# Probabilities of twelve even heads formed by rows and turned by DMA; two DRAM buffers laid out by group

## The chip, the cores and the metric

The kernel runs on one core of a Trainium2 chip. A core has TensorE (PE in the profile, with its weight loads PEld), VectorE (DVE), ScalarE (ACT), GpSimd (POOL) and SyncE (SP), which here issues nearly all DMAs, and 16 DMA engines. Each engine works off its own queue in program order. The metric is the device time of one launch in microseconds (us), the median of several runs.

## The reference

Two independent blocks, joined along the last axis. Block A is causal attention with a compressive memory: 32 heads of 18 columns, four segments of 512 positions. Block B is the real part of a two-dimensional Fourier transform by matrices.

```
# A, for every head and each of N = 4 segments of L = 512
logits = einsum("bhqd,bhkd->bhqk", qs, ks) * scale + mask
p = softmax(logits); a_dot = einsum("bhqk,bhkd->bhqd", p, vs)
pq = phi(qs); a_mem = (pq @ M) / (pq @ z + 1e-6)
o = g * a_mem + (1 - g) * a_dot
M = M + phi(ks)^T @ vs; z = z + phi(ks).sum(0)
...
a = o.reshape(B, S, D) @ wo
# B
y = dft_seq_re @ (x @ dft_hid_re.T) - dft_seq_im @ (x @ dft_hid_im.T)
```

S = 2048, D = 576. Everything is in float32; the kernel keeps that precision by splitting values in a high and a low part.

## The kernel before

**Stages.** First the projections, segment by segment (`project_qk`, `project_v`), with the memory's sums and its lookups (`lookup`); then the attention, with the Fourier matmuls woven in; last the output product. The projections leave their results in DRAM: queries and keys in `qd` and `kd`, the values' split parts in `vd[s]`, shape [128, 4, 8, 220] (row, position block j, group of four heads, columns), and the memory's part of the output in `amd[s]`, shape [4, 128, 576]. The attention reads them back by groups: `value_load` takes `vd[s][:, :, g8]`, and `memory_load` takes 72 columns of all four blocks of `amd[s]`.

**Attention.** The 128 (segment, head) pairs are numbered n = 4 G + h, with 32 groups G of four heads; groups 0 to 7 are segment 0, and so on. A generator, `attention`, makes 68 passes p. In pass p it starts the even head 2p and, with lags, carries on older heads: the odd head 2(p - 2) + 1 is filled (`F_LAG` = 2), the even head 2(p - 3) gets its transposed scores (`T_LAG` = 3), and the heads of pass p - 4 are multiplied with the values (`V_LAG` = 4). The sets of calls of a pass stand between eight yields; I call the calls ahead of yield k "block k". After each yield, the driving loop puts Fourier matmuls (the function `dense`, mostly line 583) in TensorE's queue until their share of the planned time has caught up. `later(n, ...)` puts a call off by n yields.

**An even head** goes the way by columns. `s_fill` computes its scores by rows, and DVE takes the rows' maxima from them as minima of the negated scores (line 964). `maxima` (POOL) splits the maxima of a group's two even heads in three bf16 parts. `maxima_transpose` turns these on TensorE (line 1015), ACT copies them to the tile `mt` (line 1017), and two small DMAs write them under the queries as three further rows of the contraction. `t_fill` then computes the transposed scores with the maximum already taken off (lines 1032, 1035, 1040, 1041), ACT takes the exponential twice, into f16 (`phi`) and f32 (`pf`) (lines 1044, 1045), POOL masks the diagonal blocks (`t_mask`), ACT makes their f16 part (`t_hi`) and DVE and POOL the low parts `plo` (`t_lo`). The result is already laid out as `pv` needs it.

**An odd head** goes the way by rows. `f_fill` computes the scores by rows and DVE the minima; `f_exp` adds a constant to the minima on ACT (line 984) and takes the exponential with them as bias (line 987) into `pf`; `f_split_hi` (ACT, line 994) and `f_split_lo` (POOL and DVE, line 998) make a high and a low f16 part in `hl`; `f_turn` transposes both with one DMA on SyncE's queue (line 1003) into `ptt`. `pv` multiplies with the values (lines 1076, 1077), and `pv_out` (DVE) scales and adds the memory's part.

**Banks and buffers.** Scores lie in four PSUM banks: `bank(name, shape, dtype, tag)` gives the two of tag "s" or the two of tag "t" in turn. A new tile in a bank waits for all readers of the one before it. `s_fill` and the odd head's fills 1 and 2 use "s"; `t_fill` and the odd head's fill 0 use "t". In a pass with a group's maxima to turn, `t_fill(.., 1, G)` gives `maxima_transpose` the unused last quarter of its own bank; only in pass 2, where no head is that far, the maxima take a "t" bank of their own (`trm`). `pf` has three buffers, `phi`, `plo`, `ptt` and `hl` two each.

Of the kernel before, what the change touches and what calls it, by code (L numbers as in the profile page):

```python
# [23 lines left out]
P = 128  # L24
# [11 lines left out]
COPIES = ((0, 3, 2, 0), (1, 3, 2, 2), (0, 5, 1, 0), (1, 5, 1, 1))  # L36
COPY_ROWS = 144


@with_exitstack  # L40
def infini_attention_and_fnet(ctx: ExitStack, tc: tile.TileContext, xT, wqk, w8, wv, wo, beta, xtT, cT, hT, out):
# [9 lines left out]
    kd = [dram.tile([D, 6, L], BF16, name=f"kd{s}") for s in range(NSEG)]  # L51
    vd = [dram.tile([P, 4, 8, 220], BF16, name=f"vd{s}") for s in range(NSEG)]
    amd = [dram.tile([4, P, D], F32, name=f"amd{s}") for s in range(NSEG)]
    yd = [dram.tile([P, D], F32, name=f"yd{t}") for t in range(NT)]
# [254 lines left out]
    def project_v(s, j, meanwhile):  # L309
# [26 lines left out]
        pool.tensor_tensor(vs[:, :, 0:18], r, vs[:, :, 36:54], OP.subtract)  # L336
        later(1, dma, vd[s][:, j], vs.rearrange("p (g h) c -> p g (h c)", g=8))

# [51 lines left out]
    def lookup(s, j):  # L390
# [26 lines left out]
        pool.tensor_tensor(am, nd[:, :, :DH], w.to_broadcast([P, H, DH]), OP.mult)  # L417
        later(1, dma, amd[s][j], am.rearrange("p h d -> p (h d)"))
        yield
# [73 lines left out]

    def value_load(G):
        if G < NG:
            s, g8 = divmod(G, 8)
            VS[G] = sa.tile([P, 4, 220], BF16, name="vst", bufs=2)
            dma(VS[G], vd[s][:, :, g8])

# [489 lines left out]
    def f_split_hi(n):  # L989
        f = F_[n][1]  # L990
        hl = sa.tile([P, 2, 1280], F16, name="hl", bufs=2)
        F_[n][2] = hl
        for a, b in ((512, 1280), (0, 512)):
            act.activation(hl[:, 0, a:b], f[:, a:b], AF.Copy)  # L994
# [5 lines left out]
    def f_turn(n):  # L1000
        hl = F_.pop(n)[2]
        PT[n] = sa.tile([P, 20, P], F16, name="ptt", bufs=2)
        nc.sync.dma_start_transpose(PT[n], hl.rearrange("p a c -> p (a c)"))

# [56 lines left out]
    def pv(n):  # L1061
        G, h = divmod(n, 4)
        if h % 2 == 0:
            PV[n // 2] = ps.tile([P, 448], F32, name="pv", bufs=1)
        pt = PT.pop(n)
        for i in range(4):
            o = PV[n // 2][:, (h % 2 * 4 + i) * 55:(h % 2 * 4 + i + 1) * 55]
            for j in range(i + 1):
                if h % 2:
                    b = FIRST_COL[i] // P + j  # L1070
                    hi, lo = pt[:, b], pt[:, 10 + b]
# [4 lines left out]
                pe.matmul(o, hi, v, start=j == 0, stop=False)  # L1076
                pe.matmul(o[:, 18:], lo, v[:, 18:], start=False, stop=j == i)  # L1077
# [57 lines left out]
    NP = 2 * NG  # L1135
    SLOTS = (1060.0, 890.0, 1060.0, 660.0, 890.0, 1060.0, 650.0, 1210.0)

    def attention():
        for p in range(NP + V_LAG):
            def even(lag, fn, *a):  # L1140
                if 0 <= p - lag < NP:
                    fn(2 * (p - lag), *a)

            def odd(lag, fn, *a):
# [33 lines left out]
            odd(F_LAG, f_fill, 0)  # L1178
            if p % 2 and p < NP:
                maxima(p // 2)  # L1180
# [95 lines left out]
```

## Time and profile before

| | |
|---|---|
| median of 3 runs | 993.38 us (992.39 to 993.64) |
| the profiled execution | 994.13 us; its span 992.4 us; granted clock 0.999 |
| TensorE busy | 980.9 us (99%) |
| weight loads | 918.3 us |
| VectorE | 786.4 us |
| ScalarE | 714.7 us |
| GpSimd | 675.2 us |
| moved by DMA | 209.97 MB in 304351 packets, 204992 of them under 512 bytes |
| DMA transposes | 64, 3.0 to 6.3 us each on SyncE's queue |

Times within the profile are counted from the span's start. The attention's scores run from 221 us to 917 us. In the timeline a row gives the start, the length, the engine, the line and the operation, `out<-in`, and in brackets how long the engine was idle before it and what ended that. A matmul's length is longer than the time that it keeps the next one from starting, so the distance of two starts is the cost of a matmul in a full queue. For an instruction of SyncE the length is the time that its queue was busy issuing the DMA, not the transfer.

### The profile page before, as it was taken

What the parts mean: (1) busy time and instruction counts of PE and PEld (TensorE: products, weight loads), DVE (VectorE), ACT (ScalarE), POOL (GpSimd) and SP (SyncE); (2) the same over time, 40 slices, a digit from 0 to 9 for tenths busy, and PEclk for the clock granted to TensorE, in tenths of its full rate; (3) what the DMA queues carried; (4) which work ended last, traced back from release to release, by engine and by line L of the source; (5) the groups of instructions that cost most, each with busy time, mean ns of one, the idle gap of its engine ahead of it and who ended that gap; (6) DMA issues with size and microseconds to landing.
All of it is one profiled execution on the core that took longest, in us unless ns stands there. A gap on an engine that the chain in (4) does not pass through costs nothing.

```text
span 992.4 us, 25495 instructions
## 1 busy us (share of the span) xinstructions
PE 980.9 (99%) x9246; PEld 918.3 (93%) x9246; DVE 786.4 (79%) x2115; ACT 714.7 (72%) x1687; POOL 675.2 (68%) x744
## 2 busy tenths in 40 slices
PE   9999999999999999999999999999999999999998
PEld 8988989898999999999999999999999999999998
DVE  6657668584678787887898878888888898989985
ACT  6757576563888777877878788886777778788442
POOL 2657576686676667676775777767676667887561
PEclk9999999999999999999999999999999999999999
DMA  7537556777578898899999998779999999988663
GB/s 241 191 117 244 194 170 241 238 243 214 146 179 206 224 239 227 203 226 241 223 253 242 235 211 191 187 196 218 247 231 219 224 241 252 249 200 180 168 199 112
DMA packets 304351, 209.97 MB, mean 212 GB/s; under 512 B 204992, under 2 KB 259136, under 8 KB 304192
## 3 DMA queue, kind: packets, MB, share of 16 engines
q1 hardware_dynamic: 304000, 208.20, 80.9%
q8 instruction: 72, 1.18, 0.5%
q14 instruction: 55, 0.45, 0.1%
q10 hardware_dynamic: 224, 0.14, 0.0%
HBM read 122.37 MB, written 58.98 MB: 183 GB/s over the span
## 4 chain that ended last, share of the span: by engine, by line
PE 84%; DVE 7%; ACT 4%; DMA 2%; issue 2%; POOL 1%; SPq 0%; POOLq 0%; DVEq 0%; ACTq 0%
PE d L583 38%; PE s L958 7%; PE v L84 4%; PE pv L1076 4%; PE qk L250 4%; PE d L628 3%; PE d L629 3%; PE d L630 3%; PE t L861 2%; PE pv L1077 2%; PE m L363 1%; PE d L861 1%; PE s L861 1%; PE t L1032 1%; PE qk L84 1%
## 5 line engine op out<-in xcount | busy, mean ns | idle before, releaser
L964 DVE CUSTOM_DVE_ANT_0 s<-s,causal 128x128 f32<-128x128 f32 (+3 forms) x512 | 248.4, 503 | 94.2 <-PE s L958 85.0
L456 POOL TENSOR_TENSOR clo<-craw,chi 128x512 fp32r<-128x512 f32 x158 | 218.2, 1381 | 91.1 <-ACT chi L451 60.8
L583 PE MATMUL d<-wide,chi 128*128 128x288 f32 x1408 | 261.9, 303 | 0.2 <-DVE y L653 0.2
L583 PEld LDWEIGHTS d<-wide,chi 128*128 128x128 f32 x1408 | 210.6, 188 | 2.7 <-issue 0.7
L583 PE MATMUL d<-wide,clo 128*128 128x288 f32 x704 | 173.4, 313 | 0.0
L998 POOL TENSOR_TENSOR hl<-pf,hl 128x768 f16<-128x768 f32 x64 | 114.0, 1782 | 67.4 <-ACT hl L994 55.6
L958 PE MATMUL s<-ks,qs 108*128 108x128 bf16 (+3 forms) x512 | 132.9, 303 | 1.7 <-DVE negm L964 1.2
L1044 ACT ACTIVATE phi<-t 128x384 f16<-128x384 f32 x128 | 61.8, 483 | 100.1 <-PE t L1041 100.1
L987 ACT ACTIVATE pf<-s,nb 128x128 f32<-128x128 f32 (+3 forms) x256 | 128.3, 527 | 6.2
L583 PE MATMUL d<-ab,chi 128*128 128x288 f32 x640 | 123.3, 302 | 0.0
L1059 DVE TENSOR_TENSOR plo<-pf,phi 128x384 f16<-128x384 f32 (+1 forms) x128 | 122.3, 955 | 0.0
L583 PEld LDWEIGHTS d<-wide,clo 128*128 128x128 f32 x704 | 117.8, 189 | 1.4
L1045 ACT ACTIVATE pf<-t 128x384 f32<-128x384 f32 (+1 forms) x192 | 99.6, 519 | 6.6 <-PE t L1032 6.3
L451 ACT ACTIVATE chi<-craw 128x512 fp32r<-128x512 f32 x160 | 100.1, 626 | 4.0 <-DMA craw<-xtT 2.4
L583 PEld LDWEIGHTS d<-ab,chi 128*128 128x128 f32 x640 | 97.8, 188 | 0.5
L994 ACT ACTIVATE hl<-pf 128x768 f16<-128x768 f32 (+1 forms) x128 | 87.4, 729 | 2.0
L583 PE MATMUL d<-ab,clo 128*128 128x288 f32 x320 | 83.0, 308 | 0.0
L628 PE MATMUL d<-wide,chi 128*128 128x288 f32 x256 | 81.4, 318 | 0.0
L630 PE MATMUL d<-wide,clo 128*128 128x288 f32 x256 | 75.6, 296 | 0.9 <-POOL clo L456 0.9
L629 PE MATMUL d<-wide,chi 128*128 128x288 f32 x256 | 75.6, 295 | 0.0
L1059 POOL TENSOR_TENSOR plo<-pf,phi 128x384 f16<-128x384 f32 x64 | 61.7, 963 | 12.0 <-ACT pf L1045 9.1
L998 DVE TENSOR_TENSOR hl<-pf,hl 128x512 f16<-128x512 f32 x64 | 69.2, 1081 | 0.0
(285 smaller groups left out, 2521.9 us busy)
## 6 DMA issues: line engine op xcount, KB each, us to landing
craw<-cT SPq DMA_DIRECT2D x128, 256.0 KB
ks<-kd SPq DMA_DIRECT2D x32, 432.0 KB
qs<-qd SPq DMA_DIRECT2D x32, 432.0 KB
craw<-xtT SPq DMA_DIRECT2D x32, 320.0 KB
vd<-vs SPq DMA_DIRECT2D x16, 440.0 KB
vst<-vd SPq DMA_DIRECT2D x32, 220.0 KB
qd<-p SPq DMA_DIRECT2D x16, 384.0 KB
kd<-p SPq DMA_DIRECT2D x16, 384.0 KB
```

The lines of the kernel that those rows point to most:

```text
L451: act.activation(hi, raw[:, :4], AF.Copy)
L456: engine.tensor_tensor(lo, raw[:, :4], hi.bitcast(F32), OP.subtract)
L583: pe.matmul(o[h], a, b[:, h * 288:h * 288 + 288], start=start, stop=stop)
L628: pe.matmul(o, xh[:, k], wl[k][:, cs], start=k == 0, stop=False)
L629: pe.matmul(o, xh[:, k], wh[k][:, cs], start=False, stop=False)
L630: pe.matmul(o, xl[:, k], wh[k][:, cs], start=False, stop=False)
L958: pe.matmul(o[:, c:c + w], q[:, i * P:w], k[:, :w], start=True, stop=True)
L964: dve.tensor_tensor_reduce(o[:, c:c + w], o[:, c:c + w], CAUSAL[0][:, L - w:], scale=scale, scalar=-LOWEST, op0=OP.add, op1=OP.min, accum_ ...
L987: act.activation(f[:, FIRST_COL[i]:FIRST_COL[i] + w], o[:, c:c + w], AF.Exp, bias=nb[:, i:i + 1], scale=-1.0)
L998: engine.tensor_tensor(hl[:, 1, a:b], f[:, a:b], hl[:, 0, a:b], OP.subtract)
L1045: act.activation(f[:, r:r + w], o[:, :w], AF.Exp, bias=LIFT, scale=SCALE)
L1059: (pool if kind == 2 else dve).tensor_tensor(lo[:, a:b], f[:, a:b], hi[:, a:b], OP.subtract)
```

## The change

The even heads (h = 0 and 2) of groups 0, 2, 4, 6, 16 and 18, twelve heads in all, go the way by rows. For them `s_fill`, `t_fill`, `t_mask`, `t_hi`, `t_lo` fall away, as do `maxima` and `maxima_transpose` for their groups; in their place stand `f_fill` (blocks 1 and 4, all three fills in "t" banks), `f_exp` (blocks 2, 3, 5), `f_split_hi` (block 5), `f_split_lo` (block 6), all in the pass of lag 3, and `f_turn` in block 1 of the next pass. Their `pv` moves from block 3 to block 6, just ahead of the odd head's. Their high and low parts lie in a buffer of tag `pf`, and each is transposed by a DMA of its own into a tile of tag `phi` or `plo`. Where the head of lag 3 goes by rows, no transposed-score bank is there to take the next group's maxima, so `maxima_transpose` takes a "t" bank of its own, ahead of the row-wise fills.

`vd` becomes [128, 8, 4, 220] and `amd` [128, 8, 4, 72], so that what a group loads is contiguous in each row, and what a projection stores is not.

```diff
+ROWWISE_GROUPS = (0, 2, 4, 6, 16, 18)
...
-    vd = [dram.tile([P, 4, 8, 220], BF16, name=f"vd{s}") for s in range(NSEG)]
-    amd = [dram.tile([4, P, D], F32, name=f"amd{s}") for s in range(NSEG)]
+    vd = [dram.tile([P, 8, 4, 220], BF16, name=f"vd{s}") for s in range(NSEG)]
+    amd = [dram.tile([P, 8, 4, 72], F32, name=f"amd{s}") for s in range(NSEG)]
...
-        later(1, dma, vd[s][:, j], vs.rearrange("p (g h) c -> p g (h c)", g=8))
+        later(1, dma, vd[s][:, :, j], vs.rearrange("p (g h) c -> p g (h c)", g=8))
...
-        later(1, dma, amd[s][j], am.rearrange("p h d -> p (h d)"))
+        later(1, dma, amd[s][:, :, j], am.rearrange("p (g h) d -> p g (h d)", g=8))
...
-            dma(VS[G], vd[s][:, :, g8])
+            dma(VS[G], vd[s][:, g8])
...
     def f_fill(n, kind):
-        o = scores(n, kind, "s" if kind else "t")
-        if kind == 1:
+        o = scores(n, kind, "s" if kind and n % 2 else "t")
+        if n not in F_:
...
     def f_split_hi(n):
         f = F_[n][1]
-        hl = sa.tile([P, 2, 1280], F16, name="hl", bufs=2)
+        hl = (sa.tile([P, 2, 1280], F16, name="hl", bufs=2) if n % 2
+              else sa.tile([P, 2, 1280], F16, name="hle", tag="pf", bufs=3))
...
     def f_turn(n):
         hl = F_.pop(n)[2]
-        PT[n] = sa.tile([P, 20, P], F16, name="ptt", bufs=2)
-        nc.sync.dma_start_transpose(PT[n], hl.rearrange("p a c -> p (a c)"))
+        if n % 2:
+            PT[n] = sa.tile([P, 20, P], F16, name="ptt", bufs=2)
+            nc.sync.dma_start_transpose(PT[n], hl.rearrange("p a c -> p (a c)"))
+            PT[n] = PT[n][:, :10], PT[n][:, 10:]
+        else:
+            PT[n] = [sa.tile([P, 10, P], F16, name="pte", tag=tag, bufs=2) for tag in ("phi", "plo")]
+            for i, t in enumerate(PT[n]):
+                nc.sync.dma_start_transpose(t, hl[:, i])
...
-            dma(OG[G % 2], amd[s][:, :, 72 * g8:72 * g8 + 72].rearrange("q p c -> p q c"))
+            dma(OG[G % 2], amd[s][:, g8])
...
+            def turned(lag, fn, *a):
+                if 2 * (p - lag) not in ROWWISE:
+                    even(lag, fn, *a)
+
+            def rowwise(lag, fn, *a):
+                if 2 * (p - lag) in ROWWISE:
+                    even(lag, fn, *a)
...
-            even(T_LAG + 1, t_lo, 0)
+            turned(T_LAG + 1, t_lo, 0)
             odd(F_LAG + 1, f_exp, 2)
             odd(F_LAG + 1, f_split_hi)
             yield SLOTS[0]
-            G = p // 2 - 1 if p % 2 == 0 and 0 < p <= NP else None
-            even(0, s_fill, 0)
-            even(T_LAG, t_fill, 0)
-            even(T_LAG, t_fill, 1, G)
-            if G is not None and p < T_LAG:
+            rowwise(T_LAG + 1, f_turn)
+            G = p // 2 - 1 if p % 2 == 0 and 0 < p <= NP and p // 2 - 1 not in ROWWISE_GROUPS else None
+            turned(0, s_fill, 0)
+            turned(T_LAG, t_fill, 0)
+            turned(T_LAG, t_fill, 1, G)
+            if G is not None and (p < T_LAG or 2 * (p - T_LAG) in ROWWISE):
                 maxima_transpose(G, bank("trm", [P, L], F32, "t"))
+            rowwise(T_LAG, f_fill, 0)
+            rowwise(T_LAG, f_fill, 1)
             odd(F_LAG + 1, f_split_lo, pool, 512, 1280)
             yield SLOTS[1]
-            even(0, s_fill, 1)
+            turned(0, s_fill, 1)
             odd(F_LAG + 1, f_split_lo, dve, 0, 512)
+            rowwise(T_LAG, f_exp, 0)
             yield SLOTS[2]
-            even(V_LAG, pv)
-            even(0, s_fill, 2)
-            even(T_LAG, t_mask)
+            turned(V_LAG, pv)
+            turned(0, s_fill, 2)
+            turned(T_LAG, t_mask)
+            rowwise(T_LAG, f_exp, 1)
             yield SLOTS[3]
             odd(F_LAG, f_fill, 1)
-            even(T_LAG, t_fill, 2)
+            turned(T_LAG, t_fill, 2)
+            rowwise(T_LAG, f_fill, 2)
             odd(F_LAG, f_fill, 0)
...
             odd(F_LAG + 1, f_turn)
...
-            even(T_LAG, t_hi)
+            turned(T_LAG, t_hi)
+            rowwise(T_LAG, f_exp, 2)
+            rowwise(T_LAG, f_split_hi)
             yield SLOTS[5]
+            rowwise(V_LAG, pv)
             odd(V_LAG, pv)
             odd(F_LAG, f_fill, 2)
+            rowwise(T_LAG, f_split_lo, pool, 512, 1280)
+            rowwise(T_LAG, f_split_lo, dve, 0, 512)
             odd(F_LAG, f_exp, 1)
-            even(T_LAG, t_lo, 1)
-            even(T_LAG, t_lo, 2)
+            turned(T_LAG, t_lo, 1)
+            turned(T_LAG, t_lo, 2)
             yield SLOTS[6]
```

More of the change, by code (lines that the diff above doesn't have):

```diff
@@ L1068, in pv @@
             for j in range(i + 1):
-                if h % 2:
+                if h % 2 or n in ROWWISE:
                     b = FIRST_COL[i] // P + j
-                    hi, lo = pt[:, b], pt[:, 10 + b]
+                    hi, lo = pt[0][:, b], pt[1][:, b]
                 else:
@@ L1131, in memory_load @@
             s, g8 = divmod(G, 8)
-            dma(OG[G % 2], amd[s][:, :, 72 * g8:72 * g8 + 72].rearrange("q p c -> p q c"))
+            dma(OG[G % 2], amd[s][:, g8])
     F_LAG, T_LAG, V_LAG = 2, 3, 4
     NP = 2 * NG
+    ROWWISE = {4 * G + h for G in ROWWISE_GROUPS for h in (0, 2)}
     SLOTS = (1060.0, 890.0, 1060.0, 660.0, 890.0, 1060.0, 650.0, 1210.0)
@@ L1160, in attention @@
             yield SLOTS[0]
-            G = p // 2 - 1 if p % 2 == 0 and 0 < p <= NP else None
-            even(0, s_fill, 0)
-            even(T_LAG, t_fill, 0)
-            even(T_LAG, t_fill, 1, G)
-            if G is not None and p < T_LAG:
+            rowwise(T_LAG + 1, f_turn)
[4 more added lines that the diff above has]
+            if G is not None and (p < T_LAG or 2 * (p - T_LAG) in ROWWISE):
                 maxima_transpose(G, bank("trm", [P, L], F32, "t"))
+            rowwise(T_LAG, f_fill, 0)
+            rowwise(T_LAG, f_fill, 1)
             odd(F_LAG + 1, f_split_lo, pool, 512, 1280)
             yield SLOTS[1]
-            even(0, s_fill, 1)
+            turned(0, s_fill, 1)
             odd(F_LAG + 1, f_split_lo, dve, 0, 512)
+            rowwise(T_LAG, f_exp, 0)
             yield SLOTS[2]
-            even(V_LAG, pv)
-            even(0, s_fill, 2)
-            even(T_LAG, t_mask)
+            turned(V_LAG, pv)
+            turned(0, s_fill, 2)
+            turned(T_LAG, t_mask)
+            rowwise(T_LAG, f_exp, 1)
             yield SLOTS[3]
             odd(F_LAG, f_fill, 1)
-            even(T_LAG, t_fill, 2)
+            turned(T_LAG, t_fill, 2)
+            rowwise(T_LAG, f_fill, 2)
             odd(F_LAG, f_fill, 0)
-            if p % 2 and p < NP:
+            if p % 2 and p < NP and p // 2 not in ROWWISE_GROUPS:
                 maxima(p // 2)
```

## The prediction

> **What bounds the kernel now.** I read the busy times first, then the stages, then TensorE's instructions in order of time, and last what the other engines wait for. The busy times and the chain of work that ended last:
>
> ```profile
> PE 980.9 (99%) x9246; PEld 918.3 (93%) x9246; DVE 786.4 (79%) x2115; ACT 714.7 (72%) x1687; POOL 675.2 (68%) x744
> ...
> PE 84%; DVE 7%; ACT 4%; DMA 2%; issue 2%; POOL 1%; SPq 0%; POOLq 0%; DVEq 0%; ACTq 0%
> ```
>
> Stages next (columns: stretch, its length, PE, PEld, DVE, ACT and POOL busy, granted clock, DMA share, GB/s):
>
> ```profile
> 300.00:350.00 50.00, 50.00 (x551) 47.07 (x550) 40.16 (x121) 39.52 (x94) 35.18 (x40) 1.00 0.84 215
> ...
> 500.00:550.00 50.00, 50.00 (x550) 46.87 (x549) 45.60 (x130) 41.16 (x98) 34.42 (x41) 1.00 1.01 246
> ...
> 600.00:650.00 50.00, 50.00 (x516) 47.55 (x515) 40.40 (x128) 41.20 (x107) 37.46 (x44) 1.00 0.79 192
> ```
>
> In the attention stage (about 220 to 915 us) TensorE is busy all the time at full clock, even where the DMA share is 1.01. So what leaves TensorE's queue is gained at its full pitch, and any wait put into that queue is lost in full. ACT is busy 39 to 41 of 50 us there: a fifth of its time is left.
>
> **What leaves TensorE.** Two stretches of its timeline, passes 28 and 29 of the attention loop:
>
> ```profile
> 514.22 0.39 PE L1032 MATMUL t<-qs,ks 111*128 111x128 bf16 x4
> 514.44 0.33 PE L1035 MATMUL t<-qs,ks 111*128 111x384 bf16 x1
> 514.60 0.22 PE L1015 MATMUL t<-ident,mb 128*128 128x128 bf16 x1
> 514.63 0.51 PE L583 MATMUL d<-wide,clo 128*128 128x288 f32 x2
> ...
> 518.35 0.22 PE L1040 MATMUL t<-qs,ks 111*128 111x128 bf16 x1
> 518.41 0.27 PE L1041 MATMUL t<-qs,ks 111*128 111x256 bf16 x1
> 518.52 0.38 PE L958 MATMUL s<-ks,qs 108*128 108x512 bf16 x1
> ```
>
> The pitch (start to next start) counts, not the duration, since matmuls overlap. An even head's transposed scores take 514.60 - 514.22 = 0.38 us and 518.52 - 518.35 = 0.17 us: 0.55 us. Its row-wise scores exist already for the maxima; they are only computed three passes later, so they count as nothing. Twelve heads: 6.6 us. The maxima's transpose (L1015) costs 0.03 us at 514.60 and is gone six times: 0.2 us. Sum: -6.8 us, and no more, because TensorE has no idle time that the change could also remove.
>
> **What ACT gets.** Groups over the attention stage (busy us, mean ns | idle before, releaser):
>
> ```profile
> L987 ACT ACTIVATE pf<-s,nb 128x256 f32<-128x256 f32 x253 | 126.8, 526 | 6.2
> L1045 ACT ACTIVATE pf<-t 128x512 f32<-128x512 f32 x189 | 98.0, 519 | 6.6 <-PE t L1032 6.3
> L994 ACT ACTIVATE hl<-pf 128x768 f16<-128x768 f32 (+1 forms) x128 | 87.4, 729 | 2.0
> L1044 ACT ACTIVATE phi<-t 128x384 f16<-128x384 f32 x126 | 60.8, 483 | 99.4 <-PE t L1041 99.4
> L1054 ACT ACTIVATE phi<-pf 128x512 f16<-128x512 f32 x63 | 39.7, 630 | 0.8 <-POOL pf L1049 0.8
> L984 ACT ACTIVATE nb<-nb 128x2 f32<-128x2 f32 x189 | 37.5, 198 | 5.1 <-DVE nb L964 4.8
> ```
>
> A head formed by columns costs ACT (98.0 + 60.8 + 39.7) / 63 = 3.2 us; one formed by rows (126.8 + 87.4 + 37.5) / 63 = 4.0 us. So ACT has 0.8 us more per head. It had an idle gap of 99.4 / 63 = 1.6 us per pass, ahead of L1044, that could hide this. But the gap stays: the exponential of the last block now waits for DVE's minimum of it, and DVE works off the odd head's block first.
>
> **The wait that the change adds.** In pass 2G + 4 of each of the six groups G, the maxima of group G + 1 can't ride in a transposed-score bank any more. `maxima_transpose` takes a "t" bank of its own, the first row-wise fill takes the other one, and the second fill needs the first one again: it waits until ACT has copied the maxima out (`mt`). That copy stands in ACT's queue behind the odd head's last exponential and both of its `f_split_hi` copies. Behind the waiting matmul stands all of TensorE's work, and nothing hides it. How late is ACT at that point? TensorE's fill against ACT's copy, for passes 4, 8, 12, 16, 36 and 40:
>
> ```profile
> 264.48 0.39 PE L1032 MATMUL t<-qs,ks 111*128 111x128 bf16 x4
> ...
> 310.76 0.39 PE L1032 MATMUL t<-qs,ks 111*128 111x128 bf16 x4
> ...
> 351.41 0.39 PE L1032 MATMUL t<-qs,ks 111*128 111x128 bf16 x4
> ...
> 392.11 0.39 PE L1032 MATMUL t<-qs,ks 111*128 111x128 bf16 x4
> ...
> 599.22 0.39 PE L1032 MATMUL t<-qs,ks 111*128 111x128 bf16 x4
> ...
> 647.69 0.39 PE L1032 MATMUL t<-qs,ks 111*128 111x128 bf16 x4
> ```
>
> ```profile
> 267.24 0.25 ACT L1017 ACTIVATE mt<-t 24x128 bf16<-24x128 f32 x1
> ...
> 313.02 0.25 ACT L1017 ACTIVATE mt<-t 24x128 bf16<-24x128 f32 x1
> ...
> 352.34 0.25 ACT L1017 ACTIVATE mt<-t 24x128 bf16<-24x128 f32 x1
> ...
> 392.54 0.60 ACT L1045 ACTIVATE pf<-t 128x512 f32<-128x512 f32 x1 [0.41 <-PE t L1032]
> 393.04 0.25 ACT L1017 ACTIVATE mt<-t 24x128 bf16<-24x128 f32 x1
> ...
> 601.10 0.25 ACT L1017 ACTIVATE mt<-t 24x128 bf16<-24x128 f32 x1
> ...
> 649.38 0.25 ACT L1017 ACTIVATE mt<-t 24x128 bf16<-24x128 f32 x1
> ```
>
> The copy no longer has an exponential of 0.5 us (392.54 to 393.04) ahead of it, and takes 0.25 us. TensorE is at the second fill about 0.25 us after the old L1032 (the maxima's matmul, and one 512-wide fill). So the wait is (copy's start) - (L1032's start) - 0.5 us: 2.3, 1.8, 0.4, 1.4 and 1.2 us, and for pass 16, where ACT idled 0.41 us, 0.0. Sum 7.1 us if ACT is as late as now. It will be later, by its 0.8 us and by the later start of the last exponential: bounds 0 us (the 1.6 us gap swallows it) and 1.8 us (0.8 us and a DVE queue of one more us). I take 1.0 us, near the added work: 6 x 1.0 = 6.0 us. Wait in all: 13.1 us.
>
> **SyncE's queue and the transposes.** Its transposes, a part of pass 8 and a store:
>
> ```profile
> L1003 SPq DMA_TRANSPOSE ptt<-hl x64: 3037/3745/6270, 258.7 to 918.4; - x64
> ```
>
> ```profile
> 211.68 0.32 SPq L94 DMA_DIRECT2D vd<-vs  x1
> ...
> 313.30 1.56 SPq L94 DMA_DIRECT2D qs<-mt  x2
> 314.96 0.35 SPq L441 DMA_DIRECT2D craw<-cT  x1
> ...
> 316.43 3.99 SPq L1003 DMA_TRANSPOSE ptt<-hl  x1
> 320.48 0.62 SPq L498 DMA_DIRECT2D vst<-vd  x1
> ```
>
> A row-wise head adds two issues with together the size of one such transpose: 3.0 to 6.3 us of SyncE, twelve times. They stand ahead of the next group's `qs<-mt` (needed about a pass later), of chunk loads (four chunks ahead) and of the odd transpose (whose reader comes a pass later); each has several us of room, so I cost those at nothing, and up to 1 us per head if the cover is gone. The nearest reader is the head's own `pv`, in the same pass. In pass 8 TensorE comes to that place at
>
> ```profile
> 317.22 0.20 PE L1076 MATMUL pv<-vst,ptt 128*128 128x55 bf16 x1
> ```
>
> which is 6.5 us after the 310.76 of L1032, and about 5.5 us when the even `pv` and two fills no longer stand between. Issue takes 3.7 us at the median, and the packets end somewhat after it. It is close; but in the passes where `mt` is waited for TensorE comes later itself, so one wait covers the other. Value 0, bounds 0 and 1 us per head (12 us).
>
> [...]
>
> **Edits that I cost at nothing.** DVE gets one difference in place of two for such a head and POOL a wider one; neither bounds a stage. The group layout turns each value load's 512 pieces into 128, and each value store's 128 into 1024: issue of the load (0.62 us) falls toward the store's 0.32 us and the reverse, sixteen stores against 32 loads, in an idle part of SyncE's queue. If that cover is gone it costs 16 x 0.3 = 5 us of SyncE, not of TensorE. A bank wait on the second fill's exponentials, and one of the high and low parts for a `pf` buffer, can each cost up to 1.2 us per group (two exponentials of 0.53 and a bias copy of 0.20 us late); both come right after the `mt` wait and are covered by it.
>
> **Sum.** -6.8 + 13.1 = +6.3 us. The profiled execution took 994.13 us (span 992.4); 994.13 + 6.3 = 1000.4. The runs' median lies 0.75 us lower: 999.7 us. With the lateness at its bounds of 0 and 1.8 us: 993.7 and 1004.5 us.
>
> **The rivals.**
> (1) Faster. ACT is not late at the `mt` copy, so the bank is free when the second fill comes, and TensorE keeps its 6.8 us. For it: in passes 12 and 16 the copy is ready within 0.4 us already, and ACT has the 1.6 us gap. Against it: the other four passes, and that ACT gets work, not less. What stays is the bank wait on the exponentials, now without its cover, at half of its 1.2 us in six passes: 993.4 - 6.8 + 3.6 = 990.2 us. It decides when the wait is under 6.8 / 6 = 1.1 us per group.
> (2) Slower still. SyncE and the DMA engines don't keep up: 640 KB more in each of twelve passes, where the DMA share is 0.79 to 0.84 in the two stretches shown above, and `pv` waits beside `mt`. For it: transposes of up to 6.3 us where DMA is full. Against it: TensorE never waited at a share of 1.01. Six heads (the second of each group, which have no `mt` wait as cover) by 1 us: 999.7 + 6 = 1005.7 us.
> (3) Nothing comes of it: ACT's lateness doesn't grow, the wait is 7.1 us and pays back the 6.8: 993.7 us.
>
> **How the numbers follow.** A difference of 0.2% (2 us) is about what a measurement of this kernel can tell from none. Chances: the forecast 0.52 (its own range 995.5 to 1004.5 us), faster 0.24, still slower 0.14, nothing 0.10. The range over all, 988.5 to 1006.5 us, leaves out the best part of rival 1 and the upper half of rival 2. Faster by over 0.2%: 0.24; within: 0.10; slower: 0.66.
>
> **What would show it.** Right: six idle stretches of TensorE between 250 and 660 us, each ended by ACT's `mt`, 1 to 4 us long, at the second row-wise fill of passes 4, 8, 12, 16, 36 and 40; 12 x 7 + 6 = 90 transposed-score and maxima matmuls fewer; ACT busier by about 10 us; 88 transposes on SyncE where 64 were. Wrong: no such stretch ended by `mt`; or stretches ended by a transpose at `pv`, or by chunk loads, that are longer than these.

## The result, and the profile after

| | before | after |
|---|---|---|
| median | 993.51 us (992.39 to 993.99, 4 runs) | 1034.78 us (1030.24 to 1035.74, 4 runs) |
| the profiled execution | 994.13 us; span 992.4 us | 1034.97 us; span 1032.9 us |
| granted clock, mean | 0.999 | 0.983 |

The ratio is 1.041 (95% interval 1.038 to 1.044): slower, as forecast, but by 41 us where 6.3 were forecast, and far outside the range. The page of the kernel after, busy times and the chain of work that ended last:

```profile
PE 988.5 (96%) x9156; PEld 924.1 (89%) x9156; DVE 782.8 (76%) x2103; ACT 726.9 (70%) x1717; POOL 661.6 (64%) x708
...
PE 73%; ACT 10%; DVE 8%; DMA 3%; issue 3%; POOL 2%; SPq 0%; POOLq 0%; ACTq 0%; DVEq 0%
```

TensorE has the 90 matmuls fewer that were named (9246 to 9156), ACT the 12 us more (714.7 to 726.9). The chain no longer runs over TensorE for 84% but for 73% of the span. TensorE's busy time nevertheless went up, from 980.9 to 988.5 us: fewer matmuls, and slower ones. The stages show where (columns as in the prediction: TensorE busy is the first pair, the granted clock stands ahead of the DMA share):

```profile
50.00:100.00 50.00, 47.59 (x261) 41.20 (x261) 30.56 (x61) 32.89 (x74) 30.67 (x34) 0.97 0.66 166
200.00:250.00 50.00, 43.55 (x313) 42.76 (x312) 28.71 (x61) 23.57 (x59) 33.43 (x34) 0.93 0.88 236
250.00:300.00 50.00, 44.43 (x350) 41.89 (x349) 31.03 (x90) 34.84 (x92) 27.38 (x31) 0.93 0.65 144
300.00:350.00 50.00, 44.33 (x486) 41.85 (x483) 32.60 (x101) 36.01 (x85) 28.55 (x27) 0.97 0.96 206
...
500.00:550.00 50.00, 50.00 (x551) 46.94 (x550) 44.43 (x127) 41.39 (x99) 37.41 (x42) 1.00 1.06 234
600.00:650.00 50.00, 47.40 (x477) 44.96 (x476) 37.21 (x115) 39.59 (x102) 32.41 (x35) 0.97 1.01 231
```

From 500 to 550 us, where no head is formed by rows, nothing has changed (551 matmuls, 50.00 us busy). The loss lies in the stretches with row-wise heads, and in two ahead of them (50 to 100, 200 to 250 us), for which the prediction's sum has no term. In all of those shown the granted clock is below 1. What TensorE waited for, in the view of waits (us in all, times, longest):

```profile
PE s L959 <- ACT mt L1025: 13.4, 6, 2.9
PE d L631 <- POOL clo L457: 6.4, 1, 6.4
PE pv L1084 <- DMA pte<-hle: 5.9, 3, 2.2
PE s L959 <- ACT pf L988: 4.6, 6, 1.5
PE pv L1085 <- DMA pte<-hle: 3.7, 4, 1.5
PE qk L251 <- DVE xt L120: 2.3, 1, 2.3
```

Only the first row stands in the forecast's sum (13.1 us). The others are four further kinds of wait, which the sum has at nothing.

**The wait for `mt`,** in pass 8 (the timeline of all engines):

```profile
325.10 0.23 PE L1023 MATMUL trm<-ident,mb 128*128 128x128 bf16 x1
...
325.16 0.38 PE L959 MATMUL s<-ks,qs 108*128 108x512 bf16 x1
...
326.55 1.36 ACT L996 ACTIVATE hl<-pf 128x768 f16<-128x768 f32 x2
...
328.11 0.25 ACT L1025 ACTIVATE mt<-trm 24x128 bf16<-24x128 f32 x1
...
328.41 0.38 PE L959 MATMUL s<-ks,qs 108*128 108x128 bf16 x2 [2.86 <-ACT mt L1025]
```

As forecast: the maxima and one fill take both "t" banks, the second fill stands at TensorE's head until ACT, after the odd head's two high parts (`hl`, 1.36 us), has copied the maxima out.

**The clock behind it.** The same wait, in three stretches of 3.41 us one after the other:

```profile
326.25:329.66 3.41, 1.25 (x10) 1.25 (x10) 1.46 (x6) 2.85 (x7) 2.51 (x3) 1.00 1.09 256
329.66:333.07 3.41, 3.41 (x17) 3.26 (x15) 0.83 (x3) 1.56 (x4) 1.28 (x1) 0.50 1.49 151
333.07:336.48 3.41, 3.41 (x59) 3.24 (x59) 2.37 (x10) 1.42 (x3) 0.00 (x0) 1.00 0.69 191
```

TensorE was idle for 3.41 - 1.25 = 2.16 us of the first. In the second it is busy throughout, but at a clock of 0.50: 17 matmuls, where the third has 59 (some of those are short). A 288-wide matmul of line 584 follows the one before it after 0.240 us in such a stretch (median of 28) and after 0.133 us at full clock (median of 2793). So the wait of 2.9 us costs an estimated 1.7 us more at most in the next stretch (half of its 3.41 us, by the clock of 0.50). The kernel before has no such stretch while TensorE works; this one has eight.

**The row transposes,** for the second head of group 4. SyncE's queue, and then TensorE:

```profile
381.97 3.67 SPq L1006 DMA_TRANSPOSE ptt<-hl  x1
385.70 0.57 SPq L499 DMA_DIRECT2D vst<-vd  x1
386.32 1.40 SPq L262 DMA_DIRECT2D qd<-qd  x1
387.82 0.52 SPq L95 DMA_DIRECT2D od<-ogt  x1
388.45 0.37 SPq L442 DMA_DIRECT2D craw<-cT  x1
388.91 3.55 SPq L1011 DMA_TRANSPOSE pte<-hle  x2
```

```profile
382.49 1.65 POOL L1000 TENSOR_TENSOR hle<-pf,hle 128x768 f16<-128x768 f32 x1 [3.33 <-ACT hle L996]
383.35 1.33 DVE L1000 TENSOR_TENSOR hle<-pf,hle 128x512 f16<-128x512 f32 x1
...
393.05 0.20 PE L1084 MATMUL pv<-vst,pte 128*128 128x55 bf16 x1 [1.62 <-DMA pte<-hle]
394.71 0.21 PE L1085 MATMUL pv<-vst,pte 128*128 128x37 bf16 x1 [1.46 <-DMA pte<-hle]
```

The low parts are ready at 383.35 + 1.33 = 384.68 us. SyncE comes to their transposes only at 388.91 us: it still issues the odd head's transpose, and then four other DMAs that were put ahead in its queue. Of the 8.4 us from the data to the first `pv`, half is spent in the queue. The second heads of groups 2, 4 and 6 wait 2.8, 3.1 and 3.3 us so; SyncE comes to their transposes 2.4, 4.2 and 3.4 us after the low parts.

**The stores by group,** still in the projections. After, and under it before:

```profile
55.70 0.52 SPq L95 DMA_DIRECT2D vd<-vs  x1
56.31 0.62 SPq L110 DMA_DIRECT2D raw<-xT  x1
...
64.50 0.63 ACT L119 ACTIVATE xt<-raw 128x512 fp32r<-128x512 f32 x1 [6.12 <-DMA raw<-xT]
...
229.39 0.51 SPq L95 DMA_DIRECT2D amd<-am  x1
...
235.16 0.95 POOL L467 MEMSET ks<- 32x1024 f32 x1 [4.57 <-DMA amd<-am]
```

```profile
54.51 0.38 SPq L109 DMA_DIRECT2D raw<-xT  x1
...
58.27 0.63 ACT L118 ACTIVATE xt<-raw 128x512 fp32r<-128x512 f32 x1 [1.49 <-DMA raw<-xT]
...
225.58 0.32 SPq L94 DMA_DIRECT2D amd<-am  x1
...
227.79 0.95 POOL L466 MEMSET ks<- 32x1024 f32 x1 [1.00 <-DMA amd<-am]
```

SyncE pays 0.2 us more per store, less than the 0.3 us that was costed. But the load of the input `xT` issued right behind a store of the values is used 64.50 - 56.31 = 8.2 us after its issue (before: 3.8 us), and the last store of `amd` lands after 5.8 us (before: 2.2 us). TensorE waits for the first at 65.90 us (2.3 us) and, through a memset on GpSimd that reuses the memory's buffer and a low part behind it, for the second (6.4 us). Not all of the 6.4 us is the store's: 0.9 us of this wait was there before, and with the rows alone and the old layouts (run 2 below) it is 2.9 us.

**The sum.** For each trace I split the span in three: TensorE's idle time (all idle times over 0.1 us ahead of a matmul), the half clock (an estimate: half of the time in which TensorE worked at a granted clock of 0.5; by the two pitches above it is 45%, so 13 us where the table has 14.4), and what is left, which is its work at full clock and the tail behind the last matmul.

| kernel | median, us | span | idle | half clock | rest |
|---|---|---|---|---|---|
| before | 993.5 | 992.4 | 7.2 | 0.0 | 985.3 |
| after | 1034.8 | 1032.9 | 40.3 | 14.4 | 978.2 |
| after less before | 41.3 | 40.5 | +33.1 | +14.4 | -7.1 |

So the 41 us are 33 us of waits and 14 us of half clock, less 7 us of work that the change does take away. The experiments below take these apart.

### The profile page after: what moved, and what is told of

It is laid out like the page before. It is cut to its first block, busy times and chain, and to the rows that moved or that the text cites. A ratio compares the mean times of both kernels' runs of the same rounds, so it can differ in the third digit from the quotient of the medians.

```text
span 1032.9 us, 25355 instructions
## 1 busy us (share of the span) xinstructions
PE 988.5 (96%) x9156; PEld 924.1 (89%) x9156; DVE 782.8 (76%) x2103; ACT 726.9 (70%) x1717; POOL 661.6 (64%) x708
## 4 chain that ended last, share of the span: by engine, by line
PE 73%; ACT 10%; DVE 8%; DMA 3%; issue 3%; POOL 2%; SPq 0%; POOLq 0%; ACTq 0%; DVEq 0%
PE d L584 32%; PE s L959 6%; PE qk L251 4%; PE pv L1084 4%; PE v L85 3%; PE d L631 3%; PE qk L85 3%; PE d L629 3%; PE d L630 3%; ACT pf L988 2%; PE t L862 2%; PE pv L1085 2%; DVE s L965 1%; PE d L862 1%; PE s L862 1%
## 5 line engine op out<-in xcount | busy, mean ns | idle before, releaser
L965 DVE CUSTOM_DVE_ANT_0 s<-s,causal 128x512 f32<-128x512 f32 (+3 forms) x512 | 246.8, 505 | 111.4 <-PE s L959 104.5
L584 PE MATMUL d<-wide,chi 128*128 128x288 f32 x1408 | 264.2, 305 | 0.2 <-DVE y L654 0.2
L584 PE MATMUL d<-wide,clo 128*128 128x288 f32 x704 | 174.5, 315 | 0.0
L988 ACT ACTIVATE pf<-s,nb 128x128 f32<-128x128 f32 (+3 forms) x304 | 152.2, 526 | 11.2 <-DMA pte<-hle 2.9
L959 PE MATMUL s<-ks,qs 108*128 108x512 bf16 (+3 forms) x512 | 128.2, 303 | 18.3 <-ACT mt L1025 13.4
L1052 ACT ACTIVATE phi<-t 128x384 f16<-128x384 f32 x104 | 50.3, 483 | 76.7 <-PE t L1049 76.6
L1067 DVE TENSOR_TENSOR plo<-pf,phi 128x384 f16<-128x384 f32 x104 | 101.6, 976 | 0.0
L1053 ACT ACTIVATE pf<-t 128x512 f32<-128x512 f32 x156 | 81.2, 520 | 7.5 <-PE t L1040 7.5
L631 PE MATMUL d<-wide,clo 128*128 128x288 f32 x256 | 78.3, 306 | 6.4 <-POOL clo L457 6.4
L629 PE MATMUL d<-wide,chi 128*128 128x288 f32 x256 | 83.3, 325 | 0.0
L630 PE MATMUL d<-wide,chi 128*128 128x288 f32 x256 | 78.2, 306 | 0.0
L959 PEld LDWEIGHTS <-qs 108*128 108x128 bf16 x512 | 39.7, 98 | 32.0 <-issue 16.9
L1000 DVE TENSOR_TENSOR hl<-pf,hl 128x512 f16<-128x512 f32 x64 | 65.0, 1015 | 4.2 <-ACT hl L996 4.2
```

What stands on the lines that cost most here:

```text
L584: pe.matmul(o[h], a, b[:, h * 288:h * 288 + 288], start=start, stop=stop)
L629: pe.matmul(o, xh[:, k], wl[k][:, cs], start=k == 0, stop=False)
L630: pe.matmul(o, xh[:, k], wh[k][:, cs], start=False, stop=False)
L631: pe.matmul(o, xl[:, k], wh[k][:, cs], start=False, stop=False)
L959: pe.matmul(o[:, c:c + w], q[:, i * P:w], k[:, :w], start=True, stop=True)
L965: dve.tensor_tensor_reduce(o[:, c:c + w], o[:, c:c + w], CAUSAL[0][:, L - w:], scale=scale, scalar=-LOWEST, op0=OP.add, op1=OP.min, accum_ ...
```

## The experiments

Each run was compared with runs of the kernel before on the same chip (medians of 993.6 to 994.0 us).

**1. The layouts alone,** on the kernel before, then each by itself.

```diff
-    vd = [dram.tile([P, 4, 8, 220], BF16, name=f"vd{s}") for s in range(NSEG)]
+    vd = [dram.tile([P, 8, 4, 220], BF16, name=f"vd{s}") for s in range(NSEG)]
-    amd = [dram.tile([4, P, D], F32, name=f"amd{s}") for s in range(NSEG)]
+    amd = [dram.tile([P, 8, 4, 72], F32, name=f"amd{s}") for s in range(NSEG)]
...
```

Both:

> Only the two DRAM layouts are changed; all heads are formed as before. Theory S (the slow stores hold up the projection stage): TensorE waits about 2 us near 65 us and about 6 us near 230 us as in the changed kernel, and runs at half clock for some us behind each; 1002 to 1008 us. Theory D (the layouts ease the DMA engines and cost nothing; all the loss is in the attention's passes): 991 to 995 us.

The memory's alone:

> The kernel before with the layout of the memory outputs alone (amd). If the wait at 230 us comes from the store of the memory outputs, whose landing lets GpSimd clear the key stacks, it is there in full, 998 to 1001 us; if it comes from the stores of the values, it is as in the kernel before, 993 to 995 us.

The values' alone:

> The kernel before with the group layout of the values alone (stores of 440 B pieces). The memory layout alone came out at 994.8 us and both together at 999.75. Theory V (the cost of the layouts is the values' slow stores alone): 998 to 1001 us, with the wait of TensorE near 64 us of about 1.2 us that both together showed. Theory B (it needs both, because two slow kinds of stores meet): 993 to 996 us.

Measured: both 999.75 us, ratio 1.0061 (1.0040 to 1.0082); the memory's 994.78 us, 1.0008 (0.9998 to 1.0018); the values' 998.29 us, 1.0047 (1.0033 to 1.0062). So the layouts cost about 6 us by themselves, and the values' layout alone 4.7 us. That is theory V's time for the values, and nearer to S than to D for both, though under its range. In the trace of the values' layout alone the wait behind the slow store is there again, 2.28 us at 65.95 us (1.2 us expected), and with it the half clock, 3.41 us from 67.30 us on. With both it is 1.2 us at 64.34 us and brings no half clock; there the wait near 230 us is 3.9 us, with a stretch of half clock. This second wait belongs to neither layout alone: it is 1.8 us with the memory's, 1.4 us with the values' and 0.9 us before.

In the changed kernel the layouts cost more than alone: 1034.78 us against 1023.57 us without them (next run), 11 us. There the waits at their places are 2.3 us at 65.90 and 6.4 us at 237.50 us, with three stretches of half clock; of the second, 2.9 us are there without the layouts too.

**2. The row-wise heads alone,** with the old layouts (the same diff the other way round, on the kernel after).

> The twelve heads by rows, with the two old layouts. Theory S: the changed kernel less the stores' part, 1020 to 1026 us, with the six waits for the copy of the maxima and the waits for the transposes still there. Theory D: the loads in small pieces fill the DMA engines further, so at least as slow as the changed kernel, 1033 us or more.

Measured: 1023.57 us (1023.20 to 1024.37), ratio 1.0301 (1.0286 to 1.0317). Waits for `mt` 13.4 us, for the row transposes 8.6 us, for the exponentials 4.3 us; idle time 33.5 us, half clock 9.3 us. That is theory S: the rows carry 30 of the 41 us. One more of their waits lies ahead of the passes with row-wise fills: at 229.72 us TensorE waits 2.9 us for the low part `clo`, where it waited 0.9 us before. GpSimd is no later there, TensorE 2 us earlier. In the seven runs with group 0 by rows and the old layouts this wait is 2.9 us each time, in run 9, where only groups 16 and 18 go by rows, 0.9 us.

**3. The maxima in a bank of tag "s",** so that the two "t" banks stay with the fills.

```diff
-                maxima_transpose(G, bank("trm", [P, L], F32, "t"))
+                maxima_transpose(G, bank("trm", [P, L], F32, "s"))
```

> As the rows alone, but the maxima's transpose takes a bank of tag s, so that no row-wise fill waits for its copy. Theory W (the six waits are lost in full, and each makes the clock drop for 3.4 us or more): the rows alone less 13 us of waits and 6 to 9 us of half clock, 999 to 1006 us. Theory M (ACT is late anyway, so the wait moves to the next bank or to the transposed probabilities): within 5 us of the rows alone.

Measured: 1021.00 us (1017.55 to 1022.19), ratio 1.0269 (1.0246 to 1.0292). TensorE's waits now:

```profile
PE s L959 <- ACT pf L988: 8.0, 10, 1.6
PE pv L1085 <- DMA pte<-hle: 7.1, 6, 1.5
PE pv L1084 <- DMA pte<-hle: 5.8, 4, 2.0
...
PE trm L1023 <- ACT pf L988: 1.3, 2, 0.7
```

The wait for `mt` is gone, 13.4 us, and the time falls by 2.6 (theory W had 999 to 1006 us). As theory M has it, the wait moved: to the exponentials (4.3 to 8.0 us, and 1.3 us before the maxima's own matmul), and to the transposes (8.6 to 12.9 us); my reading is that TensorE now comes earlier to a `pv` whose data are no earlier. The `mt` wait was the one place where the forecast saw a wait, and it was also the cover of a part of two others.

**4. Without the twelve heads' transposes.** The kernel of run 3; the high and low parts go into the buffers that the transposes would fill, and `pv` reads them as they are, so the twelve heads' products are taken with untransposed probabilities.

```diff
-            PT[n] = [sa.tile([P, 10, P], F16, name="pte", tag=tag, bufs=2) for tag in ("phi", "plo")]
-            for i, t in enumerate(PT[n]):
-                nc.sync.dma_start_transpose(t, hl[:, i])
+            PT[n] = [t.rearrange("p (b q) -> p b q", q=P) for t in hl]
```

> As the maxima in s, but the twelve heads' transposes are left out: the product with the values reads the untransposed high and low parts, which lie in the phi and plo buffers, so this part of the computation is not done. Theory T (what is left is the transposes' lateness, about 10 us of waits and 2 to 4 us of half clock): 12 us or so under the maxima in s, 988 to 994 us, so at or under the kernel before. Theory A (ACT is the bound of these passes): within 3 us of the maxima in s.

Measured: 1000.76 us (1000.36 to 1001.29), ratio 1.0070 (1.0053 to 1.0086), 20 us under run 3. This is more than the 12.9 us of waits at `pv`. Between the two profiled executions lie 16.2 us of span: idle time falls from 29.9 to 17.2 us, as much as the waits at `pv`, half clock from 5.1 to 3.4 us, and 1.9 us is in the rest. The other 4 us no trace shows: the profiled execution of run 3 was its fastest (clock 0.995; the three others 0.987 to 0.993). The edit also takes the transposes out of SyncE's queue and away from the `pf` buffers, for which ACT waited 1.8 us in run 3, so it is not the waits at `pv` alone that it tests. Theory A (within 3 us of run 3) falls; of T the mechanism holds, and what is left keeps the time above its range. What is left of the change's waits are those for the exponentials, 8.0 us in ten, the longest of them in the timeline:

```profile
607.54 0.84 ACT L988 ACTIVATE pf<-s,nb 128x128 f32<-128x128 f32 x2
608.43 0.38 PE L959 MATMUL s<-ks,qs 108*128 108x512 bf16 x1 [1.71 <-ACT pf L988]
```

The odd head's fill needs the bank that ACT is still reading for the row-wise head. The prediction costed this wait at nothing, since the `mt` wait would cover it.

**5. The high parts off ACT.** The kernel of run 4 with the twelve heads' high parts copied by GpSimd and VectorE. As in run 4, these heads' probabilities are not transposed.

```diff
-            act.activation(hl[0][:, a:b] if n % 2 == 0 else hl[:, 0, a:b], f[:, a:b], AF.Copy)
+            if n % 2:
+                act.activation(hl[:, 0, a:b], f[:, a:b], AF.Copy)
+            else:
+                (pool if a else dve).tensor_copy(hl[0][:, a:b], f[:, a:b])
```

> As the kernel without the twelve heads' transposes (the product reads untransposed parts), and their high parts are copied by GpSimd and VectorE instead of ScalarE. Theory A (what is left of the waits, about 10 us, comes from ACT being late with the exponentials): 4 to 7 us under the kernel without transposes, 993 to 997 us. Theory V (the exponentials wait for VectorE's minima, which now come later): the same or slower, 1000 us or more.

Measured: 994.01 us (991.28 to 994.71, 10 runs), ratio 0.9994 (0.9985 to 1.0003). The waits for the exponentials fall from 8.0 to 3.9 us, and idle time in all from 17.2 to 12.0 us. So theory A holds: what ACT has to do does come out on TensorE, by way of the banks. The edit takes more off ACT than the change had added (busy 726.7 to 711.2 us, 714.7 before the change), so it does not price the added work by itself. With this and without the transposes the change's own saving just pays for what is left.

**6. TensorE kept busy in the `mt` wait.** The kernel of run 2 with 30 matmuls of ones, whose results nobody reads, ahead of the second fill. If the half clock comes from idling, it goes away at these places.

```diff
+            if G is not None and 2 * (p - T_LAG) in ROWWISE:
+                o = ps.tile([P, 448], F32, name="pv", bufs=1)
+                for _ in range(30):
+                    pe.matmul(o[:, :P], ones, ones, start=True, stop=True)
```

> As the rows alone, with 30 matmuls of ones into a free bank between the first and the second row-wise fill of the six passes in which the second one waits for the copy of the maxima: they fill 1.7 us of each wait of 1.9 to 2.9 us with work that nobody reads. Theory C (an idle TensorE is clocked down for 3.4 us or more, and that is a cost of its own beside the wait): the waits shrink to about 1 us, the half-clock stretches behind them vanish, and the kernel gets 3 to 7 us faster than the rows alone although it does more, 1016 to 1021 us. Theory N (the half clock is only a mark of the idle time): the same time as the rows alone, within 1.5 us, or slower.

Measured: 1025.57 us (1025.11 to 1029.19), ratio 1.0326 (1.0307 to 1.0344). The half clock did go away at the three of these six places that have it in run 2 (265.86, 320.47 and 627.67 us; here none comes there), but not from the kernel: six stretches, at 230.62, 336.43, 373.98, 387.63, 435.42 and 971.31 us, four of them behind waits for transposes, which grew from 8.6 to 11.3 us. The added matmuls are 10 us of work, and they waited 4.0 us for the bank of `pv`. In time nothing is gained: theory C's range is missed, and the time is theory N's, 2.0 us over run 2. That idling brings the half clock is borne out, that filling it pays is not.

**7. The row transposes earlier in SyncE's queue.** The kernel of run 2, with the copies of queries and keys and the value loads put off, so that they no longer stand ahead of the transposes.

```diff
-                later(39, value_load, p // 2 + 1)
+                later(43, value_load, p // 2 + 1)
-                    later(2, copy_parts, 2, 8 + p // 2)
+                    later(5, copy_parts, 2, 8 + p // 2)
-                later(2, copy_parts, 3, (p - 4) // 2)
+                later(5, copy_parts, 3, (p - 4) // 2)
```

> As the rows alone, with the copies of query and key parts and the value loads issued three and four yields later, so that they stand behind the row-wise heads' transposes in SyncE's queue and not ahead. Theory Q (the transposes are late because SyncE is still issuing other DMAs when the low parts are ready): the waits at the product with the values of the second heads of groups 2, 4 and 6 shrink by 2 us each, with less half clock, 1013 to 1019 us. Theory E (the transposes are late because the DMA engines are full): the same waits, within 2 us of the rows alone.

SyncE's queue at the place shown above, now:

```profile
370.41 3.41 SPq L1006 DMA_TRANSPOSE ptt<-hl  x1
373.92 0.53 SPq L95 DMA_DIRECT2D od<-ogt  x1
374.54 1.59 SPq L442 DMA_DIRECT2D craw<-cT  x1
376.23 3.18 SPq L1011 DMA_TRANSPOSE pte<-hle  x2
379.46 0.71 SPq L262 DMA_DIRECT2D qd<-qd  x1
380.23 0.59 SPq L499 DMA_DIRECT2D vst<-vd  x1
```

The copy and the value load now stand behind. The waits at `pv` fall from 8.6 to 4.1 us: for the second heads of groups 2 and 4 from 2.3 and 2.7 us to 0.3 and 0.4 us, so the queue's order was a cause of these, as theory Q has it. For group 6 the wait stays, 2.6 and 2.7 us; there SyncE still comes 3.2 us after the low parts, behind the odd head's transpose and three short DMAs. And the time is 1023.91 us (1022.56 to 1024.72), ratio 1.0300 (1.0284 to 1.0315): as in run 2, and outside theory Q's range. Where it went shows in the split: idle 33.5 to 30.5 us, half clock 9.3 to 11.5 us. Two waits as long as in run 2, 2.87 us at 229.25 and 1.89 us at 964.47 us, brought no half clock there and bring it here; the last section shows what decides that.

**8. All that is computed, with each wait met at its place:** runs 3, 5 and 7 together, with the transposes, and the twelve heads' `pv` one block later; and **9.** the same with only groups 16 and 18 by rows (the last two lines below).

```diff
-            rowwise(V_LAG, pv)
             odd(V_LAG, pv)
...
             odd(F_LAG, f_exp, 0)
+            rowwise(V_LAG, pv)
...
-ROWWISE_GROUPS = (0, 2, 4, 6, 16, 18)
+ROWWISE_GROUPS = (16, 18)
```

> Row-wise heads with the old layouts, and all that is computed: the maxima turned in an s bank, the twelve heads' high parts made by GpSimd and VectorE, the copies and value loads later in SyncE's queue, and the twelve heads' pv one block later. Theory A (the waits are separate and each is mended at its place): no wait for mt, waits for exponentials of about 5 us in all, waits for the row transposes of under 3 us in all, 994 to 1000 us. Theory M (what is mended in one place comes back in the next, because low parts made after POOL's high parts are later still): waits for the row transposes of 6 us and more, half clock behind some of them, 1005 to 1013 us.

> The same with groups 16 and 18 alone formed by rows (four heads): 2.2 us of transposed scores less, and a sixth of the maxima. Theory A: waits of under 2 us in all behind 560 us, 992 to 994.5 us, so at best a gain that is barely told from none. Theory M: waits of 3 us and more with a half-clock stretch, 995 to 999 us.

Measured: with all six groups 1009.18 us (1005.64 to 1011.21), ratio 1.0151 (1.0129 to 1.0172); with two 992.09 us (991.43 to 994.60, 11 runs), ratio 0.9987 (0.9978 to 0.9997). The waits of the first:

```profile
PE pv L1088 <- DMA pte<-hle: 6.7, 6, 2.3
PE s L959 <- ACT pf L988: 4.0, 8, 1.0
...
PE pv L1087 <- DMA pte<-hle: 1.9, 3, 1.0
```

Theory M has it for six groups: the transposes are late again, by 8.6 us in all, although their reader is later. For the second heads of groups 2 and 4 the odd head's own transpose still stands ahead in SyncE's queue, and SyncE comes to theirs 4.1 and 5.1 us after the low parts; for the first heads of groups 4 and 6 it comes 0.8 and 1.7 us after them, and from there to the end of the wait 7.6 and 9.1 us go by. That GpSimd makes the high parts too, before the low ones, may add to it; by how much was not measured. Theory A has it for two: the waits that its four heads bring come to 2.1 us, just over its 2 us, the half clock to 0 while TensorE works. In groups 16 and 18 the transposes had come in time in the changed kernel too. That the difference lies in the copies of queries and keys, which SyncE issues only in passes below 36, is my reading; no run put those copies into the later passes.

Run 9 is the one kernel here whose interval lies below the kernel before, by 0.13% (0.03 to 0.22%). That is barely told from none, and under the 0.2% that the prediction took as the least to be told. It has the old layouts, a third of the change and the later copies and value loads; these by themselves were not run on the kernel before.

The split for all of them, from one profiled execution each:

| run | median, us | span | idle | half clock | rest |
|---|---|---|---|---|---|
| 1 both layouts | 999.75 | 997.4 | 10.6 | 1.7 | 985.1 |
| 1 values' layout | 998.29 | 996.6 | 10.1 | 1.7 | 984.8 |
| 1 memory's layout | 994.78 | 993.1 | 7.3 | 1.7 | 984.1 |
| 2 rows alone | 1023.57 | 1021.1 | 33.5 | 9.3 | 978.3 |
| 3 maxima in "s" | 1021.00 | 1015.4 | 29.9 | 5.1 | 980.5 |
| 4 no transposes | 1000.76 | 999.2 | 17.2 | 3.4 | 978.6 |
| 5 high parts off ACT | 994.01 | 992.2 | 12.0 | 3.4 | 976.8 |
| 6 kept busy | 1025.57 | 1027.1 | 28.4 | 10.2 | 988.6 |
| 7 transposes first | 1023.91 | 1020.7 | 30.5 | 11.5 | 978.6 |
| 8 mended, six groups | 1009.18 | 1006.0 | 21.2 | 4.5 | 980.3 |
| 9 mended, two groups | 992.09 | 990.3 | 7.9 | 0.0 | 982.5 |

The rest is 984 to 985.3 us wherever no head goes by rows, and 977 to 980.5 us where twelve do (run 6 apart, with its added matmuls): the change's gain on TensorE is there in every run, within 4 us, and nearly all the differences between the runs are waits and clock.

## Why the prediction was wrong, by its own steps

Of the waits after, 13.4 us were in the sum. The terms that it had at nothing brought 9.6 us at `pv`, 4.6 us for the exponentials and 8.7 us in the projections and just behind them (0.9 us of it there before), and the clock, which had no term, an estimated 14.4 us.

**What leaves TensorE: right in size.** Forecast -6.8 us; the rest falls by 7.1 us, and by 4.8 to 8.5 us in the other runs with twelve heads. With four heads it falls by 2.8 us, where a third of 6.6 us is 2.2. One thing was left out: the scores of group 0 "count as nothing" because they are only computed later, but TensorE comes 2 us earlier to the wait for `clo` at 229.72 us in run 2 and idles those 2 us.

**The wait for `mt`: right in place and mechanism, in its sum partly by luck.** Forecast 13.1 us in six waits of 1 to 4 us at the second fill; measured 13.4 us in six waits of 1.9 to 2.9 us. Taken singly they are more even than forecast, and the errors cancel: in pass 4, 3.3 us were forecast and 2.1 us came (with a wait of 1.5 us for an exponential just ahead), in passes 12 and 16, 1.4 and 1.0 us were forecast and 2.3 and 2.0 us came. Ahead of each of the six copies ACT works for over 3 us without a gap of more than 0.1 us, the last of it an exponential and the two high parts. So how late ACT was before did not carry over pass by pass.

**"One wait covers the other": wrong for the exponentials.** Costed at nothing; 4.6 us came, in six waits beside the `mt` ones. The bound named (1.2 us per group, 7.2 us) holds in sum, the cover does not: at 267.53 us the fill waits 0.91 us for an exponential in pass 3, in which there is no `mt` wait at all. The wait for a `pf` buffer, costed together with this one, came once: ACT waits 2.9 us for a transpose at 442.03 us, and no wait of TensorE's shows behind it.

**`pv` and the transposes: the step that failed by its reasoning.** Taken as 0, bounds 0 and 1 us per head. The 9.6 us lie within the bound of 12 us, but in three heads of 2.8 to 3.3 us and not in twelve. The prediction set the transpose's issue of 3.7 us against TensorE's 5.5 us, as if SyncE were free when the low parts are ready. The rows show it 4.2 us late there, with the odd head's transpose and four DMAs ahead. The prediction asked who stands behind the new transposes in the queue and never what stands ahead of them. That the range stopped at 1006.5 us, though its own bound on this term reached 12 us, was a further fault.

**The layouts: costed at nothing, 6 us alone and 11 us within the change.** The step said that it costs "SyncE, not TensorE". It counted issue times, and a store's did go up (0.32 to 0.51 us), and not the time until the bytes have landed: the load behind the values' store is used 8.2 us after its issue (before: 3.8 us), the memset behind the last store of `amd` is released after 5.8 us (before: 2.2 us), and TensorE waits for both. The row of the load `raw<-xT` right behind the store was in the trace of before.

**What had no step: the clock.** Waits were priced at their own length ("lost in full"). With an estimated 14.4 us the half clock is a third of the loss. The windows shown in the prediction have clock 1.00 throughout, and the only half clock in the kernel before comes behind its last matmul.

**The rivals.** The second one (SyncE and the DMA engines don't keep up, `pv` waits beside `mt`, in the second heads of groups) describes what happened at `pv` best, with its waits three times as long in half as many heads: 9.6 us where its price was 6. The first fell: the wait was 1.9 us or more in each of the six passes. The third fell with it.

## What to carry to other kernels

Price a new wait of the bottleneck engine by its own length and by what the clock does after it, and don't use one wait as the cover of another: taking the largest away here gave back 2.6 of 13.4 us. For a DMA that is put into a busy queue, count from when the data are ready through everything that stands ahead of it to the last byte, and for a changed layout look at who needs the bytes, or the next transfer, at the store's end. The work saved was there in each run with row-wise heads; it came out as time only in the kernel with four of them, 1.5 us by the medians, where hardly anything else was late.

## What the runs showed of the hardware

**Over 1.88 us of idling in a stretch of 3.41 us was enough for the half clock each time.** In the trace after, the half-clock stretches begin at 66.84, 234.09, 275.05, 329.66 us and so on, always whole multiples of 3.413 us apart: 329.66 - 275.05 = 54.61 = 16 x 3.413. Laying that grid over 13 traces (before, after and the eleven runs), its start in each taken from that trace's own half-clock stretches, and adding TensorE's idle time in each stretch: of the 33 stretches with more than 1.88 us of idle time each was followed by one at half clock; of 18 with 1.6 to 1.88 us eight were; below 1.6 us one, and it lay itself within half clock. In the trace after alone it is eight of eight above 1.88 us, two of five with 1.73 to 1.82 us, and none below. So a wait that the grid's edge cuts in two cost nothing more here (2.88 us ending at 229.72 us in run 2: 1.46 us idle in the one stretch, 1.41 in the next), and one that left 2.16 us idle within one stretch (326.25 to 329.66 us in the trace after) had a stretch at 0.50 behind it, an estimated 1.7 us more. Where a wait falls against the grid shifts with everything ahead of it; that is my reading of run 7, which had 3.0 us less idle time and 2.2 us more half clock than run 2. An example of a stretch with 1.76 us idle, and the one after it, still at full clock:

```profile
343.32:346.73 3.41, 1.65 (x13) 1.41 (x11) 1.38 (x6) 2.98 (x8) 3.41 (x4) 1.00 1.37 159
346.73:350.14 3.41, 2.37 (x49) 2.27 (x50) 0.85 (x4) 0.04 (x1) 0.28 (x1) 1.00 1.19 274
```

Single waits of 1.9 to 2.9 us sufficed for it: in these traces it is the idle share of a stretch, about half (1.88 of 3.41 us), and not a gap of its whole length.

**Small pieces moved from loads to stores.** The count of packets under 512 bytes is the same with the values' layout alone as before it, 204992, since 440-byte pieces were loaded before and are stored now; their mean time is close too (30.6 ns as loads, 29.9 ns as stores; 34.0 ns as stores in the kernel after). What changed is when: they now stand in the projections, where a load right behind them is needed at once (`raw<-xT`, 8.2 us from issue to use against 3.8 us), and no longer in the attention, where loads have a pass of room.
